# Attention, a gated layer and a rational layer in one kernel: PSUM tiles of one bank, sums of weights in place, sums of tokens in pieces

## The chip, the cores and the metric

The kernel runs on one core of a Trainium2 chip. The metric is the time of one execution on the device in microseconds. Its engines are called TensorE (PE; PEld is its weight load), VectorE (DVE), ScalarE (ACT), GpSimd (POOL) and SyncE (SP), which issues most DMAs.

## The reference

Chunked attention, a gated layer behind a root-mean-square norm, and a layer with a rational function, in float32:

```python
# q, k, v: [8 batches, 8 heads, 576, 64], chunks of 64
scores = scale * (q_c @ k_c.T)                      # per chunk
attn = exp(scores - max); attn /= sum(attn) + 1e-9
x = (attn @ v_c) laid out as [4608 tokens, 512]
xn = x / sqrt(mean(x * x) + 1e-6) * rms_g
x = (silu(xn @ w_gate) * (xn @ w_val)) @ w_out      # 512 -> 1536 -> 512
h = x @ w_in                                        # 512 -> 2048
P = a0 + a1*h + a2*h**2 + a3*h**3
Q = 1 + |b0|*|h| + |b1|*h**2
out = (P / (Q + 1e-6)) @ w_out2                     # 2048 -> 512
```

## The kernel before

Every matrix product runs as three passes over a high and a low part in fp32r (`PASSES`, L390), so one tile of 512 tokens by 128 columns with a depth of 512 takes 12 matmuls (`gemm1`, L392). Tokens come in tiles of 128 (36 of them) and in blocks of 512 (nine).

*Opening* (`manual_schedule`, L590): the string `START` gives the order of steps of generators by letter: `0` to `4` are the first token tiles (attention through `products`, `softmax`, `normalize`, `transposes`), `a` to `g` are pieces of the first three of six units of gate and value weights, loaded raw, unpacked into high and low parts by ACT and DVE (L92 to L106) and then written out to DRAM by SP (`wsd`, L175), and `M`, `N`, `O` are cells of block 0.

*Plain blocks* 0 to 2 (`plain`, L628): 12 cells a block. A cell (`cell`, L422) forms the gate (12 matmuls) and the value (12 matmuls) of 128 columns in one PSUM tile of two banks, `gv`; `gate_up` (L415) reads the gate with a tanh on ACT and a product on DVE (L417), another DVE product brings in the value (L434), and a DMA writes `u` to DRAM. Between cells "visits" handle one token tile each: products, a norm whose factor GpSimd computes (`ssq`), a scaling (`scale`, L386), transposes. `at_turn` and `spread` put all of this at turns, `do` runs what is due at a turn. From block 1 on the orders of ACT and DVE are held as written (`HELD`), and a scheduler orders the other engines by what is ready.

*Pair stages* t = 0, 1, 2 (L645 on): blocks 3 and 4, 5 and 6, 7 and 8 are done by seven products in place of eight (a Winograd form). That needs sums of weights, made once by `combos` (L153: one GpSimd sum of 2048 columns and four of 512 for each of the six units; an ACT copy and a DVE subtraction split them; SP writes them to `wsd`), and sums of tokens, made by `right_sums` (L320: four DVE subtractions of 1024 columns, each split by ACT and GpSimd) in one go, six or seven turns before the pair's stage begins. A stage has 12 groups of five brackets (`group`, L468), three groups interleaved; each group has one two-bank tile `st` with accumulators a and b, read by ACT (L474) and by DVE sums (L478).

*Output stage* (w_out, 1296 matmuls) and the *second layer* (3456 matmuls) follow and end the program.

PSUM has four two-bank buffers, taken in turn by `gv`, `st`, `xs` (products), `tp` (transposes) and the accumulators of the output stage (`pair_tile`, L202):

```python
    def pair_tile(shape, name):
        return ps_pool[0].tile(list(shape), F32, tag="pp", bufs=4, name=name)
    ...
        t = pair_tile([P, 2, W], f"gv{j}_{f}")
        g, vl = t[:, 0], t[:, 1]
```

Of the kernel before, what the change touches and what calls it, by code (L numbers as in the profile page):

```python
# [9 lines left out]
F32 = mybir.dt.float32  # L10
# [9 lines left out]
P = 128  # L20
# [6 lines left out]
    "120c31230a041b0d01e002001012c21c02cc3011021c310320130123013230a3212a31321432aa13424a213a43"  # L27
    "2bM3bb2b432d3bcMbdMMd4dMMdefg4N4deMeNgMeNMeggNNefOffNgfOggNgOggfOgOgOgO"
# [3 lines left out]
COMBOS_AT = (12, 15, 18, 21, 24, 27)  # L32
# [3 lines left out]
def fused_kernel(  # L36
# [113 lines left out]

    def combos(g):
# [6 lines left out]
        h = f32.rearrange("p (f m) (k c) -> p f m k c", f=2, k=2)  # L158
        a11, a12, a21, a22 = (h[:, f, :, k] for f in range(2) for k in range(2))
        s = s.rearrange("p (n m) (k c) -> p n m k c", n=2, k=2)  # L160
        s1, s2_, s3, s4 = (s[:, n, :, k] for n in range(2) for k in range(2))
        for o, x, y, op in ((s1, a21, a22, ALU.add), (s2_, s1, a11, ALU.subtract), (s3, a11, a21, ALU.subtract), (s4, a12, s2_, ALU.subtract)):
# [37 lines left out]
    ps_pool = [None]  # L200

    def pair_tile(shape, name):  # L202
        return ps_pool[0].tile(list(shape), F32, tag="pp", bufs=4, name=name)

    def products(x, s):
        name = f"{x.i if x else ''}_{s.i if s else ''}"
        ps = pair_tile([P, 2, 2, NP, CH], f"xs{name}")
# [62 lines left out]
    def transposes(x, p):  # L270
# [16 lines left out]
        if x:
# [6 lines left out]
            else:  # L294
# [14 lines left out]
                out=xf, in0=ps[:, 0], in1=gcol.unsqueeze(2).to_broadcast([P, KD, P]), op=ALU.mult  # L309
# [10 lines left out]
    def right_sums(t):  # L320
        raw = rawx[t]
        b11, b12, b21, b22 = (raw[:, 2 * k:2 * k + 2, h * W:(h + 1) * W] for k in range(2) for h in range(2))
        one = right[t][1]
        right[t] += [slab(f"right{t}_2", (P, 4, 2, W)), slab(f"right{t}_3", (P, 4, 2, W))]
        two, three = right[t][2:]
        place = {"B11": right[t][0][:, 0:2], "B21": right[t][0][:, 2:4], "B22": one[:, 0:2], "T1": one[:, 2:4],
                 "T2": two[:, 0:2], "T3": two[:, 2:4], "N4": three[:, 0:2]}
        wt["right", t] = place
# [564 lines left out]
```

## Time and profile before

| what | value |
|---|---|
| median of 3 runs | 1885.42 us (1884.58 to 1885.53) |
| profiled execution, device time | 1884.53 us |
| its span in the trace | 1882.7 us |
| instructions | 25535 |
| busy: PE, DVE, ACT, POOL | 1764.0, 1274.7, 988.9, 366.8 us |
| mean granted clock of PE | 0.979 |

Busy time is the time in which an engine has an instruction in work; it says nothing on how fast that instruction goes. The granted clock is a share of TensorE's full 2.4 GHz. A wait is the idle time of an engine just before an instruction, put down to what released it last.

### The profile page before, as it was taken

To read this page: it belongs to the slowest core of one execution; us is meant where nothing else is said; L and a number is where in the kernel's file an instruction comes from. 1 tells how busy PE (TensorE), PEld (TensorE's weight loads), DVE (VectorE), ACT (ScalarE), POOL (GpSimd) and SP (SyncE) were. 2 spreads that over 40 slices of the span, in tenths; PEclk is the share of its full clock that TensorE was granted. 3 is DMA by queue.
4 is the path that set the end of the run, shared out by engine and by line. 5 is a ranking of instruction groups with operands and counts; after the bars stand their busy time and mean duration, and the time that the engine had idled before them with its cause. 6 is when DMAs were issued, how large, how long until landed. Compare 5 with 4: busy or idle time off the path is not lost.

```text
span 1882.7 us, 25535 instructions
## 1 busy us (share of the span) xinstructions
PE 1764.0 (94%) x9744; PEld 1412.8 (75%) x9744; DVE 1274.7 (68%) x1831; ACT 988.9 (53%) x1623; POOL 366.8 (19%) x300
## 2 busy tenths in 40 slices
PE   6578998999799899899999999999999999999998
PEld 5467776666666677688888878888888888888887
DVE  6875655466655665644444468878787878888876
ACT  5623223233333334344444467777676776767765
POOL 0374002000200110000000123323232323323222
PEclk9789999999999999999999999999999999999999
DMA  7765643645475368396888930101011010101000
GB/s 258 267 210 195 200 137 143 228 181 216 166 290 201 123 257 334 121 331 230 272 292 298 332 130 1 46 1 45 2 44 35 11 40 6 46 0 46 0 23 23
DMA packets 109706, 272.20 MB, mean 145 GB/s; under 512 B 11024, under 2 KB 32528, under 8 KB 104336
## 3 DMA queue, kind: packets, MB, share of 16 engines
q1 hardware_dynamic: 109440, 270.32, 40.7%
q8 instruction: 76, 1.25, 0.3%
q14 instruction: 46, 0.38, 0.1%
q10 hardware_dynamic: 144, 0.26, 0.0%
HBM read 184.55 MB, written 85.98 MB: 144 GB/s over the span
## 4 chain that ended last, share of the span: by engine, by line
PE 62%; DVE 3%; ACT 1%; issue 1%; DMA 0%; POOL 0%; SPq 0%; DVEq 0%; ACTq 0%
PE o L789 21%; PE h L407 20%; PE a L714 15%; PE st L445 5%; DVE c L478 1%; ACT u L416 1%; DVE u L417 1%; DVE rawx L336 0%; DVE raw L100 0%; DMA ul<-ud 0%; ACT c L474 0%; DVE u L465 0%; DVE raw L98 0%; DVE ob L801 0%; POOL ggring L779 0%
## 5 line engine op out<-in xcount | busy, mean ns | idle before, releaser
L789 PE MATMUL o<-w,ggring 128*128 128x512 f32 x1728 | 416.6, 390 | 0.8 <-POOL ggring L779 0.6
L445 PE MATMUL st<-right,left 128*128 128x512 f32 x1512 | 383.0, 404 | 35.5 <-DVE c L478 25.5
L407 PE MATMUL h<-x,w 128*128 128x512 f32 x1728 | 414.9, 389 | 1.4 <-DVE x L725 1.4
L789 PEld LDWEIGHTS o<-w,ggring 128*128 128x128 f32 x1728 | 323.4, 188 | 71.7 <-DVE ob L803 2.8
L407 PEld LDWEIGHTS h<-x,w 128*128 128x128 f32 x1728 | 324.2, 188 | 69.2 <-DVE x L725 1.8
L445 PEld LDWEIGHTS st<-right,left 128*128 128x128 f32 x1512 | 277.2, 191 | 117.9 <-DVE c L478 34.1
L714 PE MATMUL a<-rring,w 128*128 128x512 f32 x1296 | 294.9, 389 | 2.1 <-ACT rring L689 1.3
L779 POOL TENSOR_TENSOR ggring<-T,ggring 128x512 fp32r<-128x512 f32 x144 | 187.2, 1300 | 536.4 <-PE o L789 350.3
L714 PEld LDWEIGHTS a<-rring,w 128*128 128x128 f32 x1296 | 242.9, 188 | 53.9 <-ACT rring L689 1.9
L407 PE MATMUL gv<-xT,w 128*128 128x512 f32 (+1 forms) x888 | 227.0, 410 | 35.9 <-DVE u L417 30.7
L407 PEld LDWEIGHTS gv<-xT,w 128*128 128x128 f32 x888 | 169.5, 200 | 81.0 <-DVE u L417 40.2
L758 ACT ACTIVATE V<-h 128x512 f32<-128x512 f32 x144 | 86.1, 598 | 192.6 <-PE h L407 192.6
L690 DVE TENSOR_TENSOR rring<-ul,rring 128x512 fp32r<-128x512 f32 x108 | 75.6, 700 | 140.5 <-ACT rring L689 138.5
L761 DVE SCALAR_TENSOR_TENSOR V<-V,small,R 128x512 f32<-128x512 f32 x144 | 108.3, 752 | 80.3 <-ACT R L759 80.2
L689 ACT CAST rring<-ul 128x512 fp32r<-128x512 f32 x108 | 66.9, 621 | 135.2 <-PE a L714 76.1
L565 POOL TENSOR_TENSOR x<-x2r,x 128x512 fp32r<-128x512 f32 x36 | 46.8, 1299 | 440.3 <-ACT x L564 440.3
L771 DVE SCALAR_TENSOR_TENSOR V<-V,R 128x512 f32<-128x512 f32 x144 | 99.7, 692 | 46.9 <-ACT R L770 46.9
L478 DVE TENSOR_TENSOR c<-c,st 128x512 f32<-128x512 f32 x108 | 73.4, 680 | 80.7 <-PE st L445 74.0
L772 DVE SCALAR_TENSOR_TENSOR V<-V,R 128x512 f32<-128x512 f32 x144 | 123.8, 860 | 4.9
L760 ACT ACTIVATE T<-h,small 128x512 f32<-128x512 f32 x144 | 112.6, 782 | 0.0
L773 DVE SCALAR_TENSOR_TENSOR T<-T,small,V 128x512 f32<-128x512 f32 x144 | 108.3, 752 | 5.1
L763 DVE SCALAR_TENSOR_TENSOR T<-T,small,h 128x512 f32<-128x512 f32 x144 | 107.7, 748 | 5.1
(123 smaller groups left out, 1764.9 us busy)
## 6 DMA issues: line engine op xcount, KB each, us to landing
left<-wsd SPq DMA_DIRECT2D x30, 2048.0 KB, 10.5
ud<-u SPq DMA_DIRECT2D x108, 256.0 KB, 2.2
ul<-ud SPq DMA_DIRECT2D x108, 256.0 KB, 5.6
stage<-in_w_dram SPq DMA_DIRECT2D x32, 512.0 KB, 6.5
w2d<-stage SPq DMA_DIRECT2D x32, 512.0 KB, 4.5
w<-w2d SPq DMA_DIRECT2D x8, 2048.0 KB, 10.9
wsd<-cb SPq DMA_DIRECT2D x48, 256.0 KB, 3.3
raw<-in_w_dram SPq DMA_DIRECT2D x10, 1024.0 KB, 7.8
```

Source lines behind the costliest of these rows:

```text
L407: nc.tensor.matmul(out=acc[:, ts], lhsT=w[:, wh, wk], rhs=x[:, kk, xh, ts], start=kk == 0 and n == 0, stop=kk == KD - 1 and n == 2,)
L445: nc.tensor.matmul(out=acc, lhsT=lhs[:, wh, kk * P:(kk + 1) * P], rhs=rhs[:, kk, xh, :], start=start and kk == 0 and m == 0, stop=kk == 1 ...
L478: nc.vector.tensor_tensor(out=c, in0=c, in1=of, op=ALU.add)
L714: nc.tensor.matmul(out=acc[m], lhsT=wt["o", f][:, wh, ms], rhs=r[:, xh, :], start=f == 0 and n == 0, stop=f == NF1 - 1 and n == 2,)
L760: nc.scalar.activation(out=T, in_=h, func=AF.Identity, scale=a3, bias=a2)
L761: nc.vector.scalar_tensor_tensor(out=V, in0=V, scalar=absb1, in1=R, op0=ALU.mult, op1=ALU.add)
L763: nc.vector.scalar_tensor_tensor(out=T, in0=T, scalar=a1, in1=h, op0=ALU.add, op1=ALU.mult)
L771: nc.vector.scalar_tensor_tensor(out=V, in0=V, scalar=1.0 + 1e-6, in1=R, op0=ALU.add, op1=ALU.mult)
L772: nc.vector.scalar_tensor_tensor(out=V, in0=V, scalar=-2.0, in1=R, op0=ALU.add, op1=ALU.mult)
L773: nc.vector.scalar_tensor_tensor(out=T, in0=T, scalar=a0, in1=V, op0=ALU.add, op1=ALU.mult)
L779: nc.gpsimd.tensor_tensor(out=r[:, 1, :], in0=T, in1=r[:, 0, :].bitcast(F32), op=ALU.subtract)
L789: nc.tensor.matmul(out=acc2[j][m], lhsT=r[:, rh, ms], rhs=wt["q", f][:, wh, :], start=f == 0 and n == 0, stop=f == NF2 - 1 and n == 2,)
```

## The change

- PSUM tiles of one bank: gate, value, both accumulators of a group and the four of the output stage get banks of their own (`bank`); products and transposes of attention take two-bank tiles (`two_banks`), two buffers in the opening and one afterwards. The opening has a pool of its own, closed when it ends, and the next one is opened with waits by tile.
- `combos`: GpSimd adds four pieces of 512 columns into a slab that two units share; the four sums move to DVE, in place, and copies and lows go in four pieces of 512 columns. It starts at turns 22 to 57 in place of 12 to 27, two steps a turn.
- `right_sums`: eight pieces of 512 columns; the lows move from GpSimd to DVE. For t = 0 it goes from turn 66 to turns 73 to 77, two steps a turn; later ones go over nine turns that begin 12 before the stage's end.
- `scale` moves from DVE to ACT. Visits of blocks 3 and 4 begin at turn 49 in place of 41.
- 11 slabs for 12, 21 small buffers for 13; `START` takes the loads of the later weight pieces (`e0f0g`) up.

```diff
-    "120c31230a041b0d01e002001012c21c02cc3011021c310320130123013230a3212a31321432aa13424a213a43"
-    "2bM3bb2b432d3bcMbdMMd4dMMdefg4N4deMeNgMeNMeggNNefOffNgfOggNgOggfOgOgOgO"
+    "120c31230a041b0d01e0f0g02001012c21c02cc3011021c310320130123013230a3212a31321432aa13424a213a43"
+    "2bM3bb2b432d3bcMbdMMd4dMMde4N4deMeNgMeNMeggNNefOffNgfOggNgOggfOgOgOgO"
-COMBOS_AT = (12, 15, 18, 21, 24, 27)
+COMBOS_AT = (22, 29, 36, 43, 50, 57)
...
-        return sb.tile(list(shape), dtype, tag="slab", bufs=12, name=name)
+        return sb.tile(list(shape), dtype, tag="slab", bufs=11, name=name)
...
-        return sb.tile(list(shape), F32, tag="s2", bufs=13, name=name)
+        return sb.tile(list(shape), F32, tag="s2", bufs=21, name=name)
...
-        a = slab(f"ca{g}", (P, 2, U, W), F32)
-        f32, s = a[:, 0], a[:, 1]
-        nc.gpsimd.tensor_tensor(out=f32, in0=whole[:, 0].bitcast(F32), in1=whole[:, 1].bitcast(F32), op=ALU.add)
-        yield
+        if g % 2 == 0:
+            sums[0] = slab(f"sums{g}", (P, 2, U, W), F32)
+        a = sums[0][:, g % 2]
+        for n in range(U):
+            nc.gpsimd.tensor_tensor(out=a[:, n], in0=whole[:, 0, n].bitcast(F32), in1=whole[:, 1, n].bitcast(F32), op=ALU.add)
+            yield
...
-            nc.gpsimd.tensor_tensor(out=o, in0=x, in1=y, op=op)
-            yield
-        nc.scalar.copy(b[:, 0], a[:, 1])
-        yield
-        nc.vector.tensor_tensor(out=b[:, 1], in0=a[:, 1], in1=b[:, 0].bitcast(F32), op=ALU.subtract)
-        yield
+        for o, x, y, op in ((a22, a21, a22, ALU.add), (a21, a11, a21, ALU.subtract), (a11, a22, a11, ALU.subtract), (a12, a12, a11, ALU.subtract)):
+            nc.vector.tensor_tensor(out=o, in0=x, in1=y, op=op)
+            yield
+        for n in range(U):
+            nc.scalar.copy(b[:, 0, n], a[:, n])
+            yield
+            nc.vector.tensor_tensor(out=b[:, 1, n], in0=a[:, n], in1=b32[:, 0, n], op=ALU.subtract)
+            yield
...
-    def pair_tile(shape, name):
-        return ps_pool[0].tile(list(shape), F32, tag="pp", bufs=4, name=name)
+    visits = [2]
+
+    def bank(name):
+        return ps_pool[0].tile([P, W], F32, tag="pp", bufs=8 - 2 * visits[0], name=name)
+
+    def two_banks(shape, name):
+        return ps_pool[0].tile(list(shape), F32, tag="at", bufs=visits[0], name=name)
...
-            nc.scalar.copy(hi, x)
-            nc.gpsimd.tensor_tensor(out=lo, in0=x, in1=hi.bitcast(F32), op=ALU.subtract)
-
-        for name, x, y, o in (("T1", b12, b11, b11), ("T3", b22, b12, b12), ("T2", b22, b11, b22), ("N4", b21, b22, b21)):
-            nc.vector.tensor_tensor(out=o, in0=x, in1=y, op=ALU.subtract)
-            yield
-            split(o, name)
-            yield
+        def low(o, hi, lo):
+            nc.vector.tensor_tensor(out=lo, in0=o, in1=hi.bitcast(F32), op=ALU.subtract)
+
+        last = None
+        for name, x, y, o in (("T1", b12, b11, b11), ("T2", b22, b11, b11), ("T3", b22, b12, b12), ("N4", b21, b11, b21)):
+            for k in range(2):
+                hi, lo = split(name, k)
+                nc.vector.tensor_tensor(out=o[:, k], in0=x[:, k], in1=y[:, k], op=ALU.subtract)
+                nc.scalar.copy(hi, o[:, k])
+                if last:
+                    low(*last)
+                last = o[:, k], hi, lo
+                yield
+        low(*last)
+        yield
...
-        nc.vector.tensor_scalar_mul(att[i].xa, att[i].xa, att[i].ssq)
+        nc.scalar.mul(att[i].xa, att[i].xa, att[i].ssq)
...
-        t = pair_tile([P, 2, W], f"gv{j}_{f}")
-        g, vl = t[:, 0], t[:, 1]
+        g, vl = bank(f"g{j}_{f}"), bank(f"v{j}_{f}")
...
-        ps = pair_tile([P, 2, W], f"st{t}_{q}")
-        a, b = ps[:, 0], ps[:, 1]
+        a, b = bank(f"sa{t}_{q}"), bank(f"sb{t}_{q}")
...
+        opening.close()
+        ps_pool[0] = phase.enter_context(tc.tile_pool(name="ps1", bufs=1, space=PSUM, reuse_waits="tile"))
+        visits[0] = 1
...
-            visit(B0[1] + 17 + 3 * n, 3 * TB + n, 0, 2)
+            visit(B0[2] + 1 + 3 * n, 3 * TB + n, 0, 2)
...
-        at_turn(B0[2] + 18, lambda: run(right_sums(0)))
+        spread(B0[2] + 25, right_sums(0), 1, 2, 5)
         for g in range(NG):
-            spread(COMBOS_AT[g], combos(g))
+            spread(COMBOS_AT[g], combos(g), 1, 2, 9)
...
-                    at_turn(base + len(ORDER) - 7, lambda t=t: run(right_sums(t + 1)))
+                    spread(base + len(ORDER) - 12, right_sums(t + 1), 1, 1, 9)
```

How instructions move shows in the order on three engines. First TensorE in block 2, cells 5 and 6, with its waits (`gv` is the shared tile of gate and value, `g` and `v` the separate ones, `xs` and `tp` attention's products and transposes). Before:

```order
L407 MATMUL gv2_5_2568<-xT2_1450,w2_565 128x512 x8
L216 MATMUL xs18_19_2584<-v18_2331,pT18_2551 64x64 [waits DMAHW4_49,Activation_49]
L216 MATMUL xs18_19_2584<-v18_2331,pT18_2551 64x64 x15
L216 MATMUL xs18_19_2584<-k19_2447,q19_2446 64x64 [waits DMAHW7_49,DMAHW6_49]
L216 MATMUL xs18_19_2584<-k19_2447,q19_2446 64x64 x15
L407 MATMUL gv2_6_2644<-xT2_1450,w3_628 128x512 [waits DVE_49]
L407 MATMUL gv2_6_2644<-xT2_1450,w3_628 128x512 x11
L407 MATMUL gv2_5_2568<-xT2_1450,w2_565 128x512 [waits DVE_49]
L407 MATMUL gv2_5_2568<-xT2_1450,w2_565 128x512 x11
```

In the change:

```order
L428 MATMUL g2_5_2457<-xT2_1382,w2_568 128x512 x12
L428 MATMUL v2_5_2458<-xT2_1382,w2_568 128x512 x12
L286 MATMUL tp15_16_2492<-ident_63,p16_2436 128x128 [waits PE_49,Activation_49]
L286 MATMUL tp15_16_2492<-ident_63,p16_2436 128x128 x3
L289 MATMUL tp15_16_2492<-ident_63,xa15_2429 128x128 [waits Activation_49]
L289 MATMUL tp15_16_2492<-ident_63,xa15_2429 128x128 x3
L428 MATMUL g2_6_2518<-xT2_1382,w3_636 128x512 x12
L223 MATMUL xs16_17_2535<-v16_2250,pT16_2501 64x64 [waits DMAHW7_49,DVE_49]
L223 MATMUL xs16_17_2535<-v16_2250,pT16_2501 64x64 x15
L223 MATMUL xs16_17_2535<-k17_2373,q17_2372 64x64 [waits DMAHW6_49,DMAHW5_49]
L223 MATMUL xs16_17_2535<-k17_2373,q17_2372 64x64 x15
L428 MATMUL v2_6_2519<-xT2_1382,w3_636 128x512 x12
```

Each run of twelve of a `gv` cell began with a wait for DVE; the `v` runs carry none now, and transposes and products, which share one tile, wait for each other's readers.

Second, DVE near the end of the stage t = 0, where the sums of tokens for t = 1 are made (`rawx` holds the tokens, L336 and L353 are the subtractions, L347 the lows, L478 and L497 the sums that read an accumulator). Before:

```order
L465 TENSOR_TENSOR u_8_3914<-u_8_3914,c_0_9_4132 128x512
L478 TENSOR_TENSOR c_0_10_4148<-c_0_10_4148,st_10_4063 128x512
L417 SCALAR_TENSOR_TENSOR u_10_4184<-u_10_4184,c_0_10_4148 128x512
L336 TENSOR_TENSOR rawx_3083<-rawx_3083 128x2x512 x4
L478 TENSOR_TENSOR c_0_11_4166<-c_0_11_4166,st_11_4100 128x512
L465 TENSOR_TENSOR u_10_4184<-u_10_4184,c_0_11_4166 128x512
L478 TENSOR_TENSOR c_0_9_4124<-c_0_9_4124,st_9_4043 128x512
L465 TENSOR_TENSOR u_9_3968<-u_9_3968,c_0_9_4124 128x512
```

In the change:

```order
L497 TENSOR_TENSOR c_0_11_4222<-c_0_11_4222,sb_11_4215 128x512
L485 TENSOR_TENSOR u_10_4193<-u_10_4193,c_0_11_4222 128x512
L353 TENSOR_TENSOR rawx_3188<-rawx_3188 128x512 x2
L347 TENSOR_TENSOR rightt_4233<-rawx_3188,rightt_4233 128x512
L353 TENSOR_TENSOR rawx_3188<-rawx_3188 128x512
L347 TENSOR_TENSOR rightt_4233<-rawx_3188,rightt_4233 128x512
L353 TENSOR_TENSOR rawx_3188<-rawx_3188 128x512
L347 TENSOR_TENSOR rightt_4233<-rawx_3188,rightt_4233 128x512
L497 TENSOR_TENSOR c_0_9_4250<-c_0_9_4250,sb_9_4156 128x512
L485 TENSOR_TENSOR u_8_4026<-u_8_4026,c_0_9_4250 128x512
L353 TENSOR_TENSOR rawx_3188<-rawx_3188 128x512
```

Four subtractions of 1024 columns in a row became pieces of 512, each followed by a low that GpSimd made before, with sums of the accumulators among them.

Third, the queue of SP in the opening (`raw_170` and `raw_179` are raw weights of the second and third unit; `wsd` the writes of the first one). Before:

```order
L117 DMA raw_114<-in_w_dram 128x1024 x2
L117 DMA raw_170<-in_w_dram 128x2x1024
L175 DMA wsd<-w_264 128x2x256 x5
L420 DMA ud_74<-u_0_458 128x512
L117 DMA raw_170<-in_w_dram 128x2x1024
L117 DMA raw_495<-in_w_dram 128x2x1024 x2
```

In the change:

```order
L117 DMA raw_114<-in_w_dram 128x1024 x2
L117 DMA raw_170<-in_w_dram 128x2x1024 x2
L117 DMA raw_179<-in_w_dram 128x2x1024 x2
L179 DMA wsd<-w_269 128x2x256 x5
L441 DMA ud_74<-u_0_463 128x512
```

The raw loads now stand ahead of the five writes, where the second half of `raw_170` stood behind them.

## Rows read from the trace of the kernel before

**Rows 1.** The page, part 1: busy us, share of the span, instructions.

```profile
PE 1764.0 (94%) x9744; PEld 1412.8 (75%) x9744; DVE 1274.7 (68%) x1831; ACT 988.9 (53%) x1623; POOL 366.8 (19%) x300
```

**Rows 2.** Timeline of PE (start, us, line, operation [idle before <-releaser]), 795 to 1115.

```profile
797.72 291.62 PE L714 MATMUL a<-rring,w 128*128 128x512 f32 x1284 [1.26 <-ACT rring L689]
```

**Rows 3.** Windows: us of each, then busy us of the engines, granted clock, DMA.

```profile
24.00:79.00 55.00, 38.88 (x216) 29.88 (x216) 38.26 (x51) 37.59 (x44) 0.87 (x1) 0.84 0.72 263
79.00:103.00 24.00, 13.48 (x106) 10.38 (x107) 23.88 (x18) 8.07 (x10) 22.84 (x11) 0.65 0.49 165
103.00:161.00 58.00, 42.69 (x289) 33.22 (x288) 33.49 (x40) 14.31 (x23) 37.30 (x22) 0.85 0.60 200
161.00:341.00 180.00, 166.41 (x1472) 130.45 (x1471) 106.50 (x166) 53.62 (x92) 32.09 (x33) 0.98 0.50 170
341.00:506.00 165.00, 146.52 (x1090) 109.88 (x1089) 103.05 (x161) 56.46 (x104) 17.68 (x20) 0.97 0.52 192
506.00:671.00 165.00, 144.22 (x1021) 108.25 (x1020) 100.52 (x156) 55.22 (x102) 17.66 (x20) 0.97 0.55 207
671.00:794.00 123.00, 117.63 (x494) 89.79 (x492) 73.52 (x103) 52.05 (x78) 0.00 (x0) 1.00 0.67 250
```

**Rows 4.** Timeline of PE: half-width matmuls, then the bundles of one token tile.

```profile
31.46 5.88 PE L407 MATMUL gv<-xT,w 128*128 128x256 f32 x36 [1.41 <-DVE u L417]
...
205.69 0.60 PE L278 MATMUL tp<-ident,p 128*128 128x128 f32 x4
206.12 0.60 PE L281 MATMUL tp<-ident,xa 128*128 128x128 f32 x4
...
207.68 0.69 PE L216 MATMUL xs<-v,pT 64*64 64x64 f32 x32
208.20 0.65 PE L216 MATMUL xs<-k,q 64*64 64x64 f32 x32
```

**Rows 5.** Waits of PE: for whom, us in total, times, longest.

```profile
PE gv L407 <- DVE u L417: 30.7, 21, 5.4
PE st L445 <- DVE c L478: 25.5, 17, 6.4
PE tp L278 <- ACT p L240: 16.3, 8, 7.0
```

**Rows 6.** Timeline of DVE, 77 to 103 us.

```profile
77.80 1.22 DVE L106 TENSOR_TENSOR w<-raw,w 128x1024 fp32r<-128x1024 f32 x1
...
79.74 4.72 DVE L387 TENSOR_SCALAR xa<-xa,ssq 128x512 f32<-128x512 f32 x1
...
99.05 3.95 DVE L106 TENSOR_TENSOR w<-raw,w 128x1024 fp32r<-128x1024 f32 x2
```

**Rows 7.** Single lines: duration ns min/median/max, first and last start us, forms.

```profile
L387 DVE TENSOR_SCALAR xa<-xa,ssq x32: 477/481/4718, 79.7 to 630.0; 128x512 f32<-128x512 f32 x32
...
L98 DVE TENSOR_SCALAR raw<-raw x20: 417/689/4985, 12.1 to 765.5; 128x1024 uint32<-128x1024 uint32 x16, 128x512 uint32<-128x512 uint32 x4
...
L336 DVE TENSOR_TENSOR rawx<-rawx x12: 1219/2240/3353, 318.1 to 656.1; 128x1024 f32<-128x1024 f32 x12
...
L163 POOL TENSOR_TENSOR ca<-ca x24: 1262/1460/3320, 88.8 to 178.2; 128x512 f32<-128x512 f32 x24
```

**Rows 8.** Timeline of POOL, 79 to 102 us.

```profile
79.67 9.14 POOL L155 TENSOR_TENSOR ca<-w 128x2048 f32<-128x2048 f32 x2
88.78 13.14 POOL L163 TENSOR_TENSOR ca<-ca 128x512 f32<-128x512 f32 x7
```

**Rows 9.** Timelines of DVE and PE around the second right sums.

```profile
486.14 9.12 DVE L336 TENSOR_TENSOR rawx<-rawx 128x1024 f32<-128x1024 f32 x4
...
495.92 4.47 PE L445 MATMUL st<-right,left 128*128 128x512 f32 x12 [6.44 <-DVE c L478]
```

**Rows 10.** Timelines of SP and ACT in the opening, 24 to 45 us.

```profile
24.88 5.67 SPq L175 DMA_DIRECT2D wsd<-w  x5
...
43.69 1.10 ACT L92 ACTIVATE raw<-raw 128x1024 f32<-128x1024 f32 x1 [5.72 <-DMA raw<-in_w_dram]
```

More of the change, by code (lines that the diff above doesn't have):

```diff
@@ L157, in combos @@
         b = slab(f"cb{g}", (P, 2, U, W))
-        h = f32.rearrange("p (f m) (k c) -> p f m k c", f=2, k=2)
+        b32 = b.bitcast(F32)
+        h = a.rearrange("p (f m) (k c) -> p f m k c", f=2, k=2)
         a11, a12, a21, a22 = (h[:, f, :, k] for f in range(2) for k in range(2))
-        s = s.rearrange("p (n m) (k c) -> p n m k c", n=2, k=2)
-        s1, s2_, s3, s4 = (s[:, n, :, k] for n in range(2) for k in range(2))
-        for o, x, y, op in ((s1, a21, a22, ALU.add), (s2_, s1, a11, ALU.subtract), (s3, a11, a21, ALU.subtract), (s4, a12, s2_, ALU.subtract)):
-            nc.gpsimd.tensor_tensor(out=o, in0=x, in1=y, op=op)
+        for o, x, y, op in ((a22, a21, a22, ALU.add), (a21, a11, a21, ALU.subtract), (a11, a22, a11, ALU.subtract), (a12, a12, a11, ALU.subtract)):
+            nc.vector.tensor_tensor(out=o, in0=x, in1=y, op=op)
@@ L284, in transposes @@
             p.pT = p.tmp([P, NP, P], "pT")
-            nc.scalar.copy(p.pT, ps[:, 1])
+            nc.scalar.copy(p.pT, tp)
             yield
@@ L300, in transposes @@
                     right[t].append(slab(f"right{t}_1", (P, 4, 2, W)))
+                    zero, one = right[t]
+                    wt["right", t] = {"B11": zero[:, 0:2], "B21": zero[:, 2:4], "B22": one[:, 0:2], "T3": one[:, 2:4]}
                 at = second * W + x.off
@@ L322, in right_sums, with split @@
         b11, b12, b21, b22 = (raw[:, 2 * k:2 * k + 2, h * W:(h + 1) * W] for k in range(2) for h in range(2))
[L323 to L328, printed above, removed]
-        def split(x, name):
-            hi, lo = place[name][:, :, 0], place[name][:, :, 1]
-            nc.scalar.copy(hi, x)
-            nc.gpsimd.tensor_tensor(out=lo, in0=x, in1=hi.bitcast(F32), op=ALU.subtract)
-        for name, x, y, o in (("T1", b12, b11, b11), ("T3", b22, b12, b12), ("T2", b22, b11, b22), ("N4", b21, b22, b21)):
-            nc.vector.tensor_tensor(out=o, in0=x, in1=y, op=ALU.subtract)
-            yield
-            split(o, name)
-            yield
+        place = wt["right", t]
+        def split(name, k):
+            if name in ("T1", "T2"):
+                if ("t", t) not in right:
+                    right["t", t] = slab(f"rightt{t}", (P, 4, 2, W))
+                place["T1"], place["T2"] = right["t", t][:, 0:2], right["t", t][:, 2:4]
+            elif name == "N4":
+                if ("n", t) not in right:
+                    right["n", t] = slab(f"rightn{t}", (P, 4, 2, W))
+                place["N4"] = right["n", t][:, 0:2]
+            return (place[name][:, k, n] for n in range(2))
+        def low(o, hi, lo):
[12 more added lines that the diff above has]
+        yield
     def load(i, start=False):
@@ L567, in fused_kernel @@
     with ExitStack() as phase:
-        ps_pool[0] = phase.enter_context(tc.tile_pool(name="ps1", bufs=1, space=PSUM))
+        opening = ExitStack()
+        ps_pool[0] = opening.enter_context(tc.tile_pool(name="ps0", bufs=1, space=PSUM))
         att.update((i, Tile(i, True)) for i in range(TB))
@@ L708, in fused_kernel @@
                 if f == 0:
-                    acc = [t[:, n] for t in (pair_tile([P, 2, W], f"a{j}_{m}") for m in range(2)) for n in range(2)]
+                    acc = [bank(f"a{j}_{m}") for m in range(KD)]
                 r = rs.pop(k)
```

19 lines of the change are left out of this document (10 added, 9 removed).

## The prediction, made before the changed kernel ran

> **What bounds the kernel now.** The page's table of busy time comes first: TensorE is busy 1764.0 of 1882.7 us [rows 1], so at most 118.7 us of plain idle time can be won, plus what a slow pipeline or a low clock hides inside the busy time. The timeline of TensorE says where it is not: from 797.72 us on, 1284 matmuls run in one piece of 291.62 us [rows 2], and what follows keeps the same pace; the change touches that part only in the names of its accumulators. That row also gives the price of one matmul of 512 columns when nothing holds TensorE up: 291.62 / 1284 = 0.227 us. Anything the change brings must come before 794 us.
>
> The windows view cuts that time into stages [rows 3]. The opening and block 0 are three windows up to 161 us, blocks 1 and 2 end at 341, the stages of the three pairs of blocks (t = 0, 1, 2) at 506, 671 and 794. A stage is worth the difference between its length and what its own work costs at full pace: 0.227 us per matmul, 0.163 for one of half the width (36 in 5.88 us [rows 4]), and about 2.2 us for a token tile of attention, which is two bundles of four transposes (0.43 + 0.60) and two of 32 small products (0.52 + 0.65) [rows 4].
>
> - 24 to 161: 48 half matmuls, 267 whole ones and about five tiles make 8 + 61 + 11 = 80 of 137 us: 57 lost, of them about 23 up to 79 us, 14 from there to 103, 20 behind.
> - 161 to 341: 576 matmuls and 12 tiles, 131 + 26 = 157 of 180: 23 lost.
> - t = 0 and t = 1: 504 matmuls and 8 tiles, 114 + 18 = 132 of 165: 33 lost in each.
> - t = 2: 504 matmuls, 114 of 123: 9 lost.
>
> That is 155 us in all, the most the change can win; it holds what a low clock costs too, since the granted clock is 0.65 to 0.85 of full speed up to 161 us and 0.97 to 1.00 behind [rows 3]. Who holds TensorE up is in the table of waits [rows 5]: the gate and value tile waits 30.7 us for the DVE operation that reads the gate (L417), the products 25.5 us for the sum that reads the same two-bank tile (L478), the transposes 16.3 us for a softmax that comes late. VectorE (DVE) is thus the partner to watch. It is 23.88 of 24 us busy between 79 and 103 us, while GpSimd is busy for 22.84 of them [rows 3]. What VectorE does then: one scaling of 512 columns takes 4.72 us [rows 6], where the median of that line is 0.481 [rows 7]; L98 takes up to 4.985 against 0.689 [rows 7], two L106 take 3.95, where one alone has just taken 1.22 [rows 6]. At the same moment GpSimd runs nine additions, 9.14 and 13.14 us [rows 8]. The same pair shows in the right sums: 2.240 us in the median, 1.219 at best [rows 7], four in a row 9.12 us, and TensorE's next matmul comes 6.44 us late [rows 9].
>
> **The change, part by part.**
>
> *Gate and value in banks of their own (blocks 1 and 2, block 0).* Before, one tile holds both, so the first value matmul waits until DVE has read the gate; now no value matmul carries a wait. Taken away: the 30.7 us of gate-and-value waits, of which some 12 lie up to 161 us behind data that would be late in any case. Added: attention has one tile of two banks where it had four shared ones, so transposes and products take turns in it; 12 to 24 matmuls, 2.7 to 5.4 us, stand between two users, and the readers (two DVE operations of 512 columns, half of the 1.22 that 1024 take [rows 6], or one and a copy on ACT) fit in that. DVE gets 24 sums and 24 lows of 512 columns in place of six lows of 2048, at 0.61 per 512 columns 29 us for 15. Three of those lows (7 us) and the first right sums (9 us) go from this stage, the 29 us come: 106.50 [rows 3] becomes about 119 of the 157 to 168 us that remain. I take **12 us** of the 23; bounds 0 (the single tile and DVE eat it) and 20.
>
> *The opening.* The second unit's loads are issued ahead of the six left-side writes, which hold SP for 5.67 us, and ACT's 5.72 us of waiting for raw goes [rows 10]. Between 79 and 103, 4.2 + 4.3 + 1.5 = 10 us of DVE's stretching goes if the GpSimd burst goes. Of the 22 us of additions then, about 10 come back (a burst of eight 512-column adds stands early on POOL in the new order), at the old rate of about 3 us of stretch. The unpacking of weights, which paces block 0, therefore ends near 103 - 5.7 - 10 + 3 = 90 instead of 103. Behind it, 37.30 us of GpSimd [rows 3] leave block 0 for blocks 1 and 2, and with them the stretched L167 and late softmax. I take 8 + 12 + 18 = **38 us** of the 57; bounds 15 (only the load and half of the stretching) and 52 (all but the first waits for data).
>
> *The right sums, spread.* A burst of four 1024-column subtractions plus four GpSimd lows costs TensorE 6.4 us and some 3 more in the slowed operations behind it; eight pieces of a subtraction and a low each, among other work, cost DVE some 10 us at 0.61 an operation, about what the burst takes now, and no sum waits for more than two of them. In the pair stages the two accumulators in banks of their own take most of the 25.5 us of waits. t = 1: 9 from the burst and 13 from the banks, **22**, bounds 8 and 30. t = 0: the same, but the sums for t = 0 itself move into its first turns, where T1 is needed after 9.3 us of TensorE's work (41 matmuls) and comes behind some twenty operations, 12.5 us, of DVE's; with what queues behind it that is 5 to 7 us, so **15**, bounds 0 and 25. t = 2 has only the accumulators: **3**, bounds 0 and 5.
>
> *Small things.* The scaling moves to ACT, half of the 1.10 us that 1024 columns take there [rows 10]; ACT's idle time hides it (56 of 165 us busy [rows 3]), and if that were gone, the transposes would be 0.6 us later per tile. Twenty-one small buffers, eleven slabs, later visits: no wait of TensorE [rows 5] is for a buffer of theirs, cost and gain 0; were a slab missing, a load of left parts would come late. Closing and reopening the PSUM pool has each tile wait for its own predecessor alone: 0.
>
> Sum: 38 + 12 + 15 + 22 + 3 = 90. The profiled execution took 1884.53 us (span 1882.7), 0.9 below the median of the runs shown. 1884.5 - 90 = 1794.5, and with 0.9 for the median **1795 us**. All lower bounds together give 1862, all upper ones 1753.
>
> **The rivals.**
>
> *The lock stays.* Twenty-four GpSimd additions of 512 columns remain (median 1.460 us [rows 7]), and the sums that moved are DVE operations with both operands in SBUF. If each addition stops DVE for its whole length, and DVE sets the pace in blocks 1 and 2, that is 24 x 1.46 = 35 us; the forecast's gain shrinks to about 57, **1828 us**. For it: the stretched operations [rows 6, 8]. Against it: DVE keeps about 40 us of slack there, and GpSimd was busy for 32.09 us in that stage before the change as well [rows 3]. The Trainium skill, "SBUF — State Buffer", section "Who interferes with whom", says that VectorE and GpSimd share a pair of ports under an exclusive lock, the later one blocked for a whole instruction, and that a VectorE instruction with two SBUF inputs contends with a GpSimd one that reads SBUF. By that rule the moved sums and the remaining additions block one another; the trace agrees as far as L336 goes, 1.219 us at best against 3.353 at most [rows 7].
>
> *TensorE close to its pace.* Once nothing shares a tile, all upper bounds hold: 132 us, **1753 us**. Against it: the visits' chains of ACT, DVE and GpSimd remain, and so do waits for data at the start.
>
> *The single attention tile, slower.* Transposes and products of every visit must now take turns in one tile: 32 visits, 64 alternations. If each costs TensorE more than 90/64 = 1.4 us, the gain is gone; at 2 us each, about one stretched operation of DVE ahead of the reader (2.240 [rows 7]), the time is 1884.5 + 128 - 90 + 1 = **1923 us**. For it: transposes already wait 16.3 us for softmax in eight waits [rows 5]. Against it: the order places 12 to 24 matmuls between them.
>
> *Nothing happens.* The waits could be shadows of a DVE that is simply full, and 1885 stays. Against it: DVE is busy 103 of 165 us [rows 3].
>
> **How the numbers follow.** Forecast (gain of 60 or more but not all) 0.66; lock stays 0.20; close to the pace 0.08; slower 0.04; nothing 0.02. A measurement of this kernel can tell 0.2% (3.8 us) from no change. Faster takes the first three, 0.94; same 0.02; slower 0.04. The range must hold 8 in 10: from 1755, where the close-to-pace case lies, to 1850, beyond the lock's 1828 and short of the sum of lower bounds; what lies outside is the last two cases and the tails.
>
> **What would show it.** In the windows of the changed kernel, block 0 ends near 123 us instead of 161, blocks 1 and 2 take about 168, t = 0 about 150, t = 1 about 143, t = 2 about 120; the whole part up to the output stage ends near 705 us instead of 795. Waits of the value matmuls for the gate's reader vanish, and waits for the transposes' tile stay under 20 us. No DVE operation of 512 columns takes over 4 us before 100 us. Wrong would be: DVE busy nearly all of blocks 1 and 2 with operations over 2 us (first rival), waits of transposes or products for a reader of the attention tile of 1.4 us or more (third), or a wait for T1 at the start of t = 0 above 10 us.

## The result, and the profile after

The changed kernel takes 1768.99 us (median of 4 runs, 1768.48 to 1770.03), the one before 1885.0 in the same comparison: a ratio of 0.9387, interval 0.937 to 0.9403, a gain of 116 us where 90 was forecast. 1795 was the forecast, 1755 to 1850 the range.

The page's table of busy time of the changed kernel, to be held against [rows 1]:

```profile
PE 1724.9 (98%) x9744; PEld 1413.4 (80%) x9744; DVE 1262.8 (71%) x1877; ACT 1012.7 (57%) x1685; POOL 301.0 (17%) x282
```

The span fell by 115.9 us, from 1882.7 to 1766.8. TensorE's idle time went from 118.7 to 41.9 us, which is 76.8 of them; its busy time fell by 39.1 for the same 9744 matmuls. So a third of the gain was never listed as a wait. A single matmul is busy for 0.389 us (the median of L738), one in a row adds 0.227 [rows 2], so by estimate each new start behind a pause costs some 0.16 us of busy time; and the mean granted clock rose from 0.979 to 0.996.

The windows of the changed kernel, its stages cut at its own ends; columns as in [rows 3], and the opening with block 0 in two parts:

```profile
24.00:79.00 55.00, 49.51 (x309) 40.13 (x310) 45.76 (x60) 44.03 (x58) 9.90 (x10) 0.97 0.73 268
79.00:121.00 42.00, 37.07 (x341) 29.49 (x339) 29.03 (x44) 16.03 (x28) 10.12 (x11) 0.96 0.69 232
...
121.00:279.00 158.00, 157.11 (x1433) 128.97 (x1434) 115.43 (x191) 63.34 (x120) 32.96 (x40) 1.00 0.63 220
279.00:420.00 141.00, 136.69 (x1122) 109.37 (x1121) 105.13 (x179) 66.12 (x125) 5.92 (x16) 1.00 0.60 214
420.00:558.00 138.00, 134.80 (x1020) 109.77 (x1021) 95.33 (x160) 60.76 (x115) 5.92 (x16) 0.99 0.67 247
558.00:672.00 114.00, 113.48 (x499) 92.77 (x497) 75.76 (x108) 53.65 (x80) 0.00 (x0) 1.00 0.75 282
```

Opening and block 0 take 97 us in place of 137, blocks 1 and 2 take 158 for 157 us of work, the pair stages 141, 138 and 114 in place of 165, 165 and 123. The granted clock is 0.96 or more from the start, where it was 0.65 to 0.85 up to 161 us [rows 3]. That is 122 us; the output stage and what follows gave 6 of them back (1094.8 us from 672 on, 1088.7 from 794 before).

The waits of TensorE in the changed kernel, against [rows 5]:

```profile
PE a L738 <- ACT rring L713: 5.6, 2, 4.1
PE tp L286 <- ACT p L247: 5.3, 4, 2.9
...
PE sa L465 <- DVE c L497: 2.7, 4, 0.9
...
PE g L428 <- DVE u L438: 1.4, 1, 1.4
```

The waits for the gate's reader fell from 30.7 to 1.4 us, those for the sums from 25.5 to 2.7, those for softmax from 16.3 to 5.3. A new one leads the list. The timelines of TensorE, ACT and SP at the end of the output stage show it:

```profile
699.83 247.00 PE L738 MATMUL a<-rring,w 128*128 128x512 f32 x1089
950.90 23.69 PE L738 MATMUL a<-rring,w 128*128 128x512 f32 x96 [4.06 <-ACT rring L713]
```

```profile
949.17 0.65 ACT L92 ACTIVATE stage<-stage 128x512 f32<-128x512 f32 x1 [12.43 <-DMA stage<-in_w_dram]
```

```profile
944.23 0.33 SPq L136 DMA_DIRECT2D stage<-in_w_dram  x1
```

Before, 1284 matmuls ran there without a gap [rows 2]. Now SP issues a load of raw weights (L136) only at 944.23, ACT waits 12.43 us for it, and TensorE 4.06 for what ACT has queued behind. The 96 matmuls behind that pause take 23.69 us, 1.9 more than at 0.227 each; the granted clock is 0.89 between 944 and 960 us. Those 4.06 and 1.9 us are the 6 given back.

In the opening, the same view of DVE and of GpSimd as [rows 6, 8]:

```profile
76.17 2.32 DVE L106 TENSOR_TENSOR w<-raw,w 128x1024 fp32r<-128x1024 f32 x1
...
90.10 1.21 DVE L106 TENSOR_TENSOR w<-raw,w 128x1024 fp32r<-128x1024 f32 x1
```

```profile
72.22 13.94 POOL L159 TENSOR_TENSOR sums<-w 128x512 f32<-128x512 f32 x8
```

Eight additions remain at 72 to 86 us, and DVE beside them is stretched once more (an L106 takes 2.32 us, 1.21 alone), but nothing takes over 4 us. The last L106 of the unpacking starts at 90.10 us and ends at 91.3; 90 was forecast.

### The profile page after: what moved, and what is told of

It reads as the page before. It is cut to its first block, busy times and chain, and to the rows that moved or that the text cites. A ratio compares the mean times of both kernels' runs of the same rounds, so it can differ in the third digit from the quotient of the medians.

```text
span 1766.8 us, 25629 instructions
## 1 busy us (share of the span) xinstructions
PE 1724.9 (98%) x9744; PEld 1413.4 (80%) x9744; DVE 1262.8 (71%) x1877; ACT 1012.7 (57%) x1685; POOL 301.0 (17%) x282
## 4 chain that ended last, share of the span: by engine, by line
PE 86%; DVE 4%; DMA 2%; ACT 2%; issue 1%; POOL 0%; SPq 0%; ACTq 0%; DVEq 0%
PE o L813 22%; PE h L428 22%; PE a L738 15%; PE sa L465 8%; PE sb L465 7%; PE v L428 4%; PE g L428 4%; PE xs L223 2%; DVE c L497 1%; PE tp L286 1%; PE tp L289 1%; DMA w2d<-stage 1%; DMA raw<-in_wo_dram 1%; ACT u L437 0%; DVE rawx L353 0%
## 5 line engine op out<-in xcount | busy, mean ns | idle before, releaser
L738 PE MATMUL a<-rring,w 128*128 128x512 f32 x1296 | 296.6, 391 | 6.1 <-ACT rring L713 5.6
L738 PEld LDWEIGHTS a<-rring,w 128*128 128x128 f32 x1296 | 244.1, 189 | 58.4 <-ACT rring L713 6.8
L428 PE MATMUL g<-xT,w 128*128 128x512 f32 (+1 forms) x444 | 111.5, 399 | 3.5 <-DVE u L438 1.4
L465 PE MATMUL sa<-right,left 128*128 128x512 f32 x432 | 112.5, 398 | 0.0
L465 PE MATMUL sb<-right,left 128*128 128x512 f32 x432 | 109.6, 393 | 0.4 <-DVE u L438 0.3
L428 PE MATMUL v<-xT,w 128*128 128x512 f32 (+1 forms) x444 | 107.8, 391 | 0.0
L794 ACT ACTIVATE R<-R,small 128x512 f32<-128x512 f32 x144 | 104.5, 726 | 4.7
```

Of the source, the lines that this page charges most:

```text
L428: nc.tensor.matmul(out=acc[:, ts], lhsT=w[:, wh, wk], rhs=x[:, kk, xh, ts], start=kk == 0 and n == 0, stop=kk == KD - 1 and n == 2,)
L465: nc.tensor.matmul(out=acc, lhsT=lhs[:, wh, kk * P:(kk + 1) * P], rhs=rhs[:, kk, xh, :], start=start and kk == 0 and m == 0, stop=kk == 1 ...
L738: nc.tensor.matmul(out=acc[m], lhsT=wt["o", f][:, wh, ms], rhs=r[:, xh, :], start=f == 0 and n == 0, stop=f == NF1 - 1 and n == 2,)
L794: nc.scalar.activation(out=R, in_=R, func=AF.Exp, scale=-1.0, bias=expb)
```

## Experiments

All times are medians beside runs of the kernel before on the same chip (1884.19, 1885.24 and 1883.7 us in the three sets); intervals are of the ratio to it. The change stands at 0.9387 (0.937 to 0.9403). Gaps of under 3 us between variants are inside these intervals, and only their profiles can say more.

**PSUM undone (e1_pairs).**

```diff
-        g, vl = bank(f"g{j}_{f}"), bank(f"v{j}_{f}")
+        gv = pair_tile([P, 2, W], f"gv{j}_{f}")
+        g, vl = gv[:, 0], gv[:, 1]
...
-        a, b = bank(f"sa{t}_{q}"), bank(f"sb{t}_{q}")
+        ps = pair_tile([P, 2, W], f"st{t}_{q}")
+        a, b = ps[:, 0], ps[:, 1]
```

Products, transposes and the output accumulators go back into the same four pair tiles too.

> The changed kernel with its PSUM part undone: gate and value, both accumulators of a group, and attention share four two-bank tiles again; all else stays. Theory S (the shared tile: what TensorE lost was the wait for a reader of the other half): about 60 to 75 us slower than the change, near 1835, with the waits of value matmuls and of the second accumulator back, some 40 us of them in blocks 1 and 2 and the pair stages. Rival L (the stretched DVE: the readers were late because GpSimd held them up, and late readers only show through the shared tile): 15 to 25 us slower, near 1790.

Measured: 1862.94 us, ratio 0.9884 (0.987 to 0.9899): 94 us slower than the change, more than either theory. The waits of TensorE in it:

```profile
PE gv L423 <- DVE u L433: 20.4, 23, 2.2
PE st L461 <- ACT c L490: 14.6, 23, 2.2
PE st L461 <- DVE c L494: 14.3, 17, 1.5
```

Not one of them is long (2.2 us at most, where [rows 5] had 5.4 and 6.4), but there are many, 63 in these three rows, 49.3 us together. Its windows (opening with block 0, then the pair stages), columns as in [rows 3]:

```profile
24.00:137.00 113.00, 91.88 (x622) 71.80 (x621) 75.37 (x105) 57.84 (x79) 16.99 (x16) 0.89 0.62 219
...
310.00:477.00 167.00, 144.22 (x1081) 105.52 (x1079) 106.25 (x181) 66.57 (x125) 5.94 (x16) 1.00 0.51 183
477.00:639.00 162.00, 143.83 (x1046) 106.44 (x1044) 95.64 (x161) 60.67 (x115) 5.93 (x16) 0.99 0.58 211
639.00:764.00 125.00, 119.57 (x503) 92.03 (x504) 74.94 (x107) 52.55 (x80) 0.00 (x0) 1.00 0.69 252
```

The pair stages take 167, 162 and 125 us, as long as before the change, though the sums of tokens are spread; the opening with block 0 takes 113 in place of 97. In its page TensorE is busy for 1757.7 of 1861.6 us: 62 us more idle time than in the change and 33 us more busy time, two thirds of the loss in waiting and one in pace. Rival L falls: with GpSimd's bursts gone, the shared tile still costs 94 us.

**PSUM alone on the kernel before (e6_banks_alone).** The same edit the other way round, with the opening's pool.

> The kernel before with the PSUM part of the change alone (banks for gate, value and accumulators, attention in tiles of its own, the opening's pool apart). Undoing this part cost 94 us, the other parts by themselves brought 21 to 22. Theory A (the two groups of parts add up): 94 us faster than before, near 1790. Theory B (the banks need quick readers: with the GpSimd bursts in place, the readers are late with or without banks): 50 to 70 us faster, near 1825, with the loss in blocks 0 to 2 where the sums of weights run. Theory C (the banks do little without room in VectorE): under 40 us faster, 1845 or more.

Measured: 1805.19 us, ratio 0.9579 (0.9564 to 0.9593), 80 us faster than before; between theories A and B. The four corners are 1885 before, 1805 with banks alone, 1863 with the rest alone, 1769 with both: 80 + 21 = 101 apart, 116 together. What is missing shows in the waits (the last two rows are its windows of the opening with block 0, and of blocks 1 and 2):

```profile
PE sa L448 <- DVE c L480: 12.1, 5, 5.9
PE tp L285 <- DVE xa L391: 9.9, 4, 5.1
PE g L411 <- ACT w L104: 7.7, 2, 7.5
```

```profile
24.00:145.00 121.00, 93.54 (x643) 74.04 (x642) 93.59 (x106) 61.62 (x82) 56.03 (x32) 0.86 0.65 226
145.00:310.00 165.00, 161.54 (x1446) 131.78 (x1445) 111.75 (x171) 54.57 (x93) 38.12 (x39) 0.98 0.57 196
```

Stage by stage the banks alone bring 16 us in the opening and block 0 (121 for 137), 15 in blocks 1 and 2, and 18, 21 and 11 in the pair stages (147, 144 and 112). Without the spread sums, one accumulator waits up to 5.9 us behind a burst; without the calm opening, transposes wait for a scaling (on DVE here, L391) and the first cells for weights. The rest of the change is worth 21 us without the banks and 36 with them: so part of what late readers cost shows only once the pairing is gone.

**Attention apart, pairs kept (e8_attention_apart).**

```diff
+    def pair_tile(shape, name):
+        return ps_pool[0].tile(list(shape), F32, tag="pp", bufs=4 - visits[0], name=name)
...
-        g, vl = bank(f"g{j}_{f}"), bank(f"v{j}_{f}")
+        gv = pair_tile([P, 2, W], f"gv{j}_{f}")
+        g, vl = gv[:, 0], gv[:, 1]
```

(the accumulators alike; attention keeps its own two-bank tile behind the opening)

> The changed kernel with gate and value, and both accumulators, in one two-bank tile again (three buffers), but attention in a two-bank tile of its own behind the opening; the opening has the four shared pair tiles of before. It splits the 94 us that the pairs cost. If it is the pairing of gate with value and of a with b that costs, this stays within 15 us of the kernel with all four tiles shared, or goes above it for the buffer less: 1850 to 1875. If it is that attention came between the cells in the same ring of buffers, most comes back: near 1790.

Measured: 1859.68 us, 0.9867 (0.9852 to 0.9882), 3 us from e1_pairs. It is the pairing of gate with value and of a with b that costs, not attention in the ring; nor is it the reopened pool, which this kernel keeps. Whether a pair costs by the wait for the other half's reader or by coming free later as a whole was not separated. The row of the sums has the same many short waits:

```profile
PE st L468 <- DVE c L501: 17.4, 21, 1.5
...
PE gv L430 <- DVE u L440: 14.4, 17, 2.2
```

**Four sums of weights back on GpSimd (e2_pool_sums).**

```diff
-            nc.vector.tensor_tensor(out=o, in0=x, in1=y, op=op)
+            nc.gpsimd.tensor_tensor(out=o, in0=x, in1=y, op=op)
```

> The changed kernel with the four sums of weights of each unit back on GpSimd (in place, 512 columns), at the changed kernel's turns. Theory S: under 5 us slower, near 1772, since nothing waits for a reader that is a few us late. Rival L: 24 more GpSimd additions at about 1.5 us hold DVE up; 15 to 35 us slower, near 1795, all of it between 121 and 279 us.

Measured: 1792.33 us, 0.9508 (0.9494 to 0.9522), 23 us slower, in the middle of what rival L gave, and 19 of them in the place it named, blocks 1 and 2 (4 are in block 0). But the rows tell of another mechanism. The timelines of TensorE, GpSimd and ACT, with GpSimd's run from 162 us on:

```profile
186.70 0.84 PE L289 MATMUL tp<-ident,xa 128*128 128x128 f32 x4 [4.71 <-ACT xa L408]
...
226.06 1.11 PE L289 MATMUL tp<-ident,xa 128*128 128x128 f32 x4 [8.08 <-ACT xa L408]
```

```profile
162.42 8.10 POOL L159 TENSOR_TENSOR sums<-w 128x512 f32<-128x512 f32 x5
...
178.41 6.57 POOL L166 TENSOR_TENSOR sums<-sums 128x512 f32<-128x512 f32 x5
185.07 0.19 POOL L272 TENSOR_SCALAR ssq<-ssq 128x1 f32<-128x1 f32 x1
```

```profile
185.93 0.72 ACT L408 ACTIVATE xa<-xa,ssq 128x512 f32<-128x512 f32 x1 [8.95 <-POOL ssq L273]
```

GpSimd works through sixteen additions from 162.42 to 184.98 us, and the factor of the norm (L272) stands behind them in its queue; the scaling on ACT waits 8.95 us for it, the transposes 4.71, and 8.08 behind the next sixteen additions. The window of blocks 1 and 2 in this kernel:

```profile
125.00:302.00 177.00, 162.84 (x1442) 133.16 (x1443) 101.43 (x168) 63.59 (x121) 52.53 (x56) 0.96 0.57 197
```

177 us in place of 158: 13 of the 19 more are idle time of TensorE (14.2 against 0.9), and the transposes' two waits make 12.8 of it; 6 are busy time at a lower clock, 0.96 for 1.00. So what GpSimd's additions cost there is mostly the wait of those that queue behind them. DVE was less loaded than in the change (101.43 us for 115.43).

**Right sums in one go, lows on GpSimd (e3_right_burst).**

```diff
-            nc.vector.tensor_tensor(out=lo, in0=o, in1=hi.bitcast(F32), op=ALU.subtract)
+            nc.gpsimd.tensor_tensor(out=lo, in0=o, in1=hi.bitcast(F32), op=ALU.subtract)
...
-        spread(B0[2] + 25, right_sums(0), 1, 2, 5)
+        at_turn(B0[2] + 25, lambda: run(right_sums(0)))
...
-                    spread(base + len(ORDER) - 12, right_sums(t + 1), 1, 1, 9)
+                    at_turn(base + len(ORDER) - 7, lambda t=t: run(right_sums(t + 1)))
```

> The changed kernel with the sums of tokens in one go again, seven turns before the end of a stage (for t = 0 at its old place of the new table, turn 73), and their lows on GpSimd, in pieces of 512 columns. Theory S: the banks take the burst's edge off; 5 to 10 us slower for the two bursts in t = 0 and t = 1 and some 5 for the one at the start of t = 0, near 1782. Rival L: each burst stops TensorE for 9 us and over, 25 to 30 us slower, near 1797.

Measured: 1787.05 us, 0.9478 (0.9462 to 0.9494), 18 us slower, between the two. The stage t = 0 holds two bursts and takes 154 us (141 in the change), t = 1 139, t = 2 117. Its window, and TensorE after the second burst:

```profile
280.00:434.00 154.00, 142.87 (x1126) 113.92 (x1125) 107.52 (x168) 67.30 (x126) 30.55 (x32) 0.96 0.56 204
```

```profile
427.12 1.22 PE L465 MATMUL sa<-right,left 128*128 128x512 f32 x2 [4.69 <-DVE c L497]
```

4.69 us late (and 5.35 behind the third burst, in t = 1), 6.44 before [rows 9]: with banks the burst costs less, not nothing.

**The opening's string undone (e4_start).** `START` as before.

> The changed kernel with the opening's string of before: the raw loads of the second and third unit come behind the writes of the first again. The prediction's term: ACT's wait of 5.7 us for raw comes back and the unpacking ends that much later, 5 to 7 us slower, near 1775. Rival: the unpacking is paced by DVE and ACT, whose queue has slack by now, so 0 to 2 us, near 1770.

Measured: 1776.94 us, 0.943 (0.9416 to 0.9444), 8 us slower, 6 in the profiled execution. Its waits hold one that the change has almost lost (1.3 us there), first cells for ACT's cast of weights:

```profile
PE g L428 <- ACT w L104: 6.8, 2, 6.4
```

```profile
46.63 1.10 ACT L92 ACTIVATE raw<-raw 128x1024 f32<-128x1024 f32 x1 [6.31 <-DMA raw<-in_w_dram]
```

ACT waits 6.31 us for raw again, as in [rows 10], and the last L106 ends 5.6 us later (96.9 for 91.3): the term of 5.7 us for the load is borne out at the unpacking. At the end of block 0 it is 4 us (123.6 for 119.5); some 2 of the 6 come in the output stage, where the wait near 957 us is 5.86 us in this execution, and are not the load's.

**Early sums of weights (e5_early_combos).** `COMBOS_AT = (12, 15, 18, 21, 24, 27)`.

> The changed kernel with the sums of weights at the turns of before (12 to 27). If it is their place in the opening that costs (GpSimd beside a VectorE that paces the unpacking), block 0 ends 10 to 15 us later, blocks 1 and 2 win back 2 or 3, and the kernel is 8 to 12 us slower, near 1779. If with banks of their own nobody waits for a VectorE that is a little late, 0 to 3 us slower, 1770.

Measured: 1780.46 us, 0.9451 (0.9437 to 0.9465), 11 us slower. The place of the sums does cost, but not as I thought: block 0 ends only 3 us later (its last value matmul ends at 122.1 us, 119.5 in the change), and blocks 1 and 2 lose the rest. The timelines of TensorE and DVE:

```profile
131.88 0.90 PE L223 MATMUL xs<-v,pT 64*64 64x64 f32 x18 [8.95 <-DVE xf L318]
```

```profile
125.55 3.41 DVE L171 TENSOR_TENSOR cb<-sums,cb 128x512 fp32r<-128x512 f32 x2
128.88 1.74 DVE L166 TENSOR_TENSOR sums<-sums 128x512 f32<-128x512 f32 x1
...
131.14 0.68 DVE L318 TENSOR_TENSOR xf<-tp,small 128x512 f32<-128x512 f32 x1
```

The products of a token tile wait 8.95 us for DVE to read the transposes that stand in the one attention tile (L318, at 131.14). DVE comes to it late, behind sums and lows that run beside GpSimd's third burst (two L171 in 3.41 us, some 0.69 each in calm). That is the mechanism of the third rival, at one place.

**Additions on VectorE as well (e13_adds_dve).**

```diff
-            nc.gpsimd.tensor_tensor(out=a[:, n], in0=whole[:, 0, n].bitcast(F32), in1=whole[:, 1, n].bitcast(F32), op=ALU.add)
+            nc.vector.tensor_tensor(out=a[:, n], in0=whole[:, 0, n].bitcast(F32), in1=whole[:, 1, n].bitcast(F32), op=ALU.add)
```

> The changed kernel with the 24 remaining additions of weights on VectorE too, so that GpSimd has nothing but the norm's factors up to the output stage. If GpSimd's additions still stop VectorE for their length (the rival of the prediction at its full price, 35 us, less 24 additions at 0.6 us), 10 to 20 us faster, near 1754. If most of them hide, as the windows say (158 us for 157 us of work in blocks 1 and 2), only the burst in the opening shows: 0 to 6 us faster, 1763 to 1769. If 14 us more of VectorE put it at its end: slower, up to 1780.

Measured: 1766.08 us, 0.9376 (0.9362 to 0.9391), 3 us from the change and inside its interval. The remaining 24 additions cost at most a few us where the rival of the lock gave them 35. In its timeline block 0 ends at 114.5 us (119.5 in the change), and blocks 1 and 2 take as long as there, 158 us, though DVE is busy for 122.13 of them in place of 115.43. Over the whole kernel DVE's busy time grows by only 4.3 us (1267.1 for 1262.8) for 24 more additions, some 14 us at 0.6 each: by this estimate the additions on GpSimd had stretched DVE's operations by some 10 us, which TensorE hardly noticed.

**GpSimd's order held (e11_pool_held).** `HELD` with the Pool engine, the first two sums at turns 24 and 30.

> The changed kernel with GpSimd's order held as written from block 1 on too, and the first two units of weight sums two and one turns later: the eight additions that the scheduler puts at 72 to 86 us, in the opening, become two there and the rest in blocks 1 and 2, in pieces of two and four. If the additions cost by stretching VectorE while it paces the opening, 4 to 8 us faster, near 1763. If their place does not matter, 1769. If the spread pieces hold up the factor of the norm or the sums come too late for the pair stages, slower, 1775 or more.

Measured: 1766.88 us, 0.9377 (0.9363 to 0.9391), not to be told from the change by its time. In the profile two additions stand in the opening in place of eight, block 0 ends at 114.0 us and the output stage begins at 669.5 (119.5 and 672.0 in the change).

**First loads of the output stage early (e10_u_early).** The six loads ten turns ahead of the end of t = 2, three splits at its last three turns.

> The changed kernel with the first six loads of the output stage issued ten turns before the last pair stage ends and the first three splits at its last three turns. In the changed kernel TensorE waits 5.6 us for the first splits (and 7 to 8 in three of the undone kernels). If the wait is for the loads' way and nothing else, it goes: 4 to 6 us faster than the change, near 1764. If the order of ACT behind it is what is late, no difference, 1769.

Measured: 1766.63 us, 0.9373 (0.9357 to 0.9388); its profiled execution is no shorter than the change's (span 1767.4). Inconclusive by its time. TensorE starts the output stage without a gap, but later (673.3 us), and the wait near 950 us stays, 4.66 us.

**Twelve slabs, thirteen small buffers (e12_slabs).**

> The changed kernel with twelve slabs and thirteen small buffers again. The prediction costed this edit at nothing. In the changed kernel ACT waits 12.4 us near 949 us for a stage's load that SP issued at 944, and TensorE 4.1 us for ACT behind it; before, that stretch had no gap. If the load came late for want of a slab, the gap goes and the kernel is 4 us faster, near 1765, unless thirteen small buffers cost waits in the pair stages. If the small buffers are what the new order needs, 5 us or more slower, 1774 or above. If neither matters, 1769.

Measured: 1767.42 us, 0.9388 (0.9371 to 0.9405), no difference by its time. The profile answers the question all the same:

```profile
699.75 271.94 PE L738 MATMUL a<-rring,w 128*128 128x512 f32 x1199
```

```profile
933.55 0.33 SPq L136 DMA_DIRECT2D stage<-in_w_dram  x1
```

With twelve slabs the load of raw weights is issued at 933.55 us in place of 944.23, and TensorE has no gap from 700 us to the end of the stage: the late load was a late slab. But the stage t = 0 takes 144 us (141 in the change), and the output stage begins 3 us later. Whether that is the thirteen small buffers was not separated.

**A version that beats both (e15_stage_early).** The change with e11's and e10's edits, and:

```diff
-                spread(turn_o + n * (NB * NF1 - 8) // NSTG, stage(n))
+                spread(turn_o + n * (NB * NF1 - 20) // NSTG, stage(n))
```

> A version meant to beat both: the changed kernel with GpSimd's order held and its first sums later (2 us faster by itself), the first loads of the output stage early (2 us), and the weights of the second layer staged over 88 of the 108 steps of the output stage in place of 100, so that the last of them meet free slabs. If the 4 us gap near 950 us was a slab that came late, 7 to 9 us faster than the change, near 1761; if it was DMA traffic, 3 to 5 us, near 1765; if the faster pace of staging takes too much of ACT in the output stage, no better than 1767.

Measured: 1757.38 us (1755.31 to 1759.3), 0.9328 (0.9314 to 0.9342): 11.6 us faster than the change, clear of its interval. The output stage:

```profile
666.89 293.92 PE L739 MATMUL a<-rring,w 128*128 128x512 f32 x1296
```

It begins 5 us sooner (666.9), and its 1296 matmuls run in one piece.

## Why the prediction was right, and where its sizes were off

What held is the bound and the direction; the sizes of the parts did not. Taken apart, the forecast of 90 us gave the banks 12 + 13 + 13 + 3 = 41 and the other parts 38 + 9 + 2 = 49. Alone, the banks bring 80 (e6_banks_alone) and the other parts 21 (e1_pairs); the interplay adds 15. So the banks were priced at half, the rest too high, and part of the agreement is luck. Where the banks' share was lost shows in the trace of before: of the 30.7 us that TensorE waited for the gate's reader [rows 5], the view of 24 to 161 us holds 19.5.

```profile
PE gv L407 <- DVE u L417: 19.5, 9, 5.4
```

- *What bounds the kernel*: right. The gain lies ahead of 794 us, in TensorE's waits, and 1755 to 1850 held the time. Against 155 us at most, 122 came.
- *The opening*, 38 us of 57: measured 40, but not by the causes named alone. The prediction gave the load, the stretching and GpSimd's leaving all 38 and the banks nothing there, because "some 12" of the waits for the gate's reader lay up to 161 us behind late data. By the row above, 19.5 lay there. The banks alone bring 16 us of the 40, and 24 are left for the rest. Of that rest, the load is borne out at the unpacking (5.7 forecast, 5.6 in e4_start) but only 4 us of it reach the end of block 0; the end of the unpacking is right (90 forecast, 91.3). The burst that comes back costs some 5 us of block 0 (e11_pool_held), where 3 stood.
- *Banks, blocks 1 and 2*, 12 us: measured 22, above its bound of 20. The step that failed is "the single tile and DVE eat it", for which 11 of the 23 were held back: DVE has 115.43 us of work there (119 forecast), and TensorE has 0.9 us idle in 158. By e6_banks_alone the banks alone bring 15 (165 us for 180).
- *Pair stages*, 15 + 22 + 3 = 40 us: measured 24 + 27 + 9 = 60, the last above its bound of 5. I priced the banks by the waits that are listed [rows 5], and t = 2 at 3 of its 9. Alone, they bring 18, 21 and 11 us in these stages (e6_banks_alone); undone, they cost 26, 24 and 11 (e1_pairs against the change). The wait at the start of t = 0 for T1 (5 to 7 us) was 0.6: sums and TensorE's work kept pace. The right sums by themselves are worth 18 us of the whole (e3_right_burst), for three bursts, where the forecast had 9 each for two.
- *Small things*, 0: the eleventh slab cost 4 us of waiting near 950 us, shown by e12_slabs, and 1.9 of slower matmuls behind it; the prediction had named a late load as its price, but of left parts. The 2 us of waits at the start of the output stage (0.42 + 1.57) were there before too (0.87 + 1.26). The move of the scaling to ACT was not tried by itself; with the scaling on DVE, transposes wait 9.9 us for it in e6_banks_alone.
- *The lock stays*, 1828: not so. e13_adds_dve leaves it a few us at most. The rule of the Trainium skill ("SBUF — State Buffer", "Who interferes with whom") holds for the single operation, DVE's L106 at 2.32 us beside an addition and 1.21 alone, yet DVE's slack takes it up. It cost where DVE or GpSimd had someone behind them: e2_pool_sums and e5_early_combos.
- *The single attention tile*: it did not decide in the change, whose waits of products for L318 are 1.6 us in all, the longest 1.40 and thus just at the 1.4 that was to be the sign of it; in e5_early_combos it cost 9 us at one place.
- *Close to the pace*, 1753: the change came 16 us short of it, and the extended version stands at 1757.
- Two slips in the working decide nothing: the rows show five writes ahead of the loads, not six [rows 10], and 90 less 35 is 55, so the lock's time comes to 1830.

## What to carry to other kernels

Where two results share one PSUM tile, as gate and value did here, a run of matmuls into the one waits for the readers of the other, and the table of waits tells only part of the price: compare a stage's length with its work at full pace, as the idle time was two thirds here and longer busy time the rest. Causes hide one another: while the pairing stood, the other parts brought 21 us; without it, 36. And a sum can come out near while its parts are wrong, so undo each part by itself and compare stage by stage. When an engine with slack is given bulk work, look at the short operations that queue behind it before looking at ports.

## What was not expected of the hardware

Many short pauses of TensorE cost half of their sum again in pace: e1_pairs, whose listed waits are 0.8 us each in the mean, has 62 us more idle time than the change (103.9 against 41.9) and 33 us more busy time for the same 9744 matmuls. The granted clock explains little of it: in the pair stages, where it is 1.00, 0.99 and 1.00 in both kernels, 38 us more idle time come with 23 more of busy time. And sixteen additions on GpSimd held up two operations of 0.19 and 0.55 us for so long that TensorE lost 4.71 us at that place and 8.08 behind the next sixteen.
